# A new written-out order of tasks, and six tiles for output in place of four, in a fused sparse attention and maxout kernel

## The chip, the cores and the metric

The kernel runs on one core of a Trainium2 chip. The core has TensorE (PE: matmuls; PEld is its loading of weights), VectorE (DVE), ScalarE (ACT), GpSimd (POOL) and SyncE (SP), which here only issues DMA transfers. Each engine works through its own instructions strictly in order and waits where data are not ready. The metric is the device time of one execution in microseconds (us); lower is better.

## The reference

Two parts follow each other. The first is attention over 4 batches, 8 heads, 768 positions and a head size of 64. Each query sees the keys closer than 16 positions and, besides, one summary for each block of 32 positions: the largest value of the block's keys, element by element, and the mean of its values.

```python
k_sum = k.reshape(B, H, nb, block, D).max(axis=3)
v_sum = v.reshape(B, H, nb, block, D).mean(axis=3)
scores_l = scale * np.matmul(q, k.transpose(0, 1, 3, 2))
mask_l = np.abs(pos[:, None] - pos[None, :]) < window
scores_s = scale * np.einsum('bhsd,bhnd->bhsn', q, k_sum)
scores_s = scores_s + np.log(block)
scores_l_m = np.where(mask_l, scores_l, -1000000000.0)
scores_all = np.concatenate([scores_l_m, scores_s], axis=-1)
...
return np.matmul(a, v_all).astype(np.float32)      # a: softmax of scores_all
```

Its result, 3072 tokens of 512 numbers, is the input x of a maxout layer with 1024 hidden units:

```python
h1 = x @ w1
h2 = x @ w2
g = np.maximum(h1, h2)
return (g @ w_out).astype(np.float32)
```

All inputs and the output are float32 in HBM; the kernel multiplies in bfloat16.

## The kernel before, in words

**Maxout.** The kernel uses max(h1, h2) = h1 + max(h2 − h1, 0). So it keeps wd = w2 − w1, computes x·wd (*hidden*), takes max(·, 0) on the way out of PSUM (*relu*), and multiplies by w_out. The share of h1 goes through a product w1·w_out, made once (*w1o*, from w1 turned, *w1t*). A batch has three groups of 256 tokens. For each group there are four *hidden* tasks of 8 matmuls (L660), four *relu* tasks, and for each half of 128 tokens an *output*: three steps of 4 matmuls that add into one PSUM bank (L674 with w1o, then L681 twice with w_out), a *copy out* from PSUM to a tile `o` in SBUF (L410 through the helper `copy`), and a *store* from there to HBM (L692). The tiles `o` form a ring, L202; it has four tiles. A copy into a tile must wait until the store that last read it has landed.

**Attention.** For each batch and pair of heads, k and q are loaded in float32 into a landing tile (`land`, a ring of eight; L305), *cast* to bfloat16 (`kqb`), *turned* on TensorE (L434), and *placed* from PSUM into `kx` and `qx` (L410); for k the block maxima (*max*, L454), their copies (*sums*, L461) and a *wrap* (L458) follow on DVE. *Scores* (L501) go to PSUM, *exp* (L515, ACT) to a tile `pb`, and in batches 1 to 3 a *mask* (L509, DVE) clears what is out of the window; in batch 0 TensorE adds the mask itself. v is loaded in two halves (L327), cast to `vb`, and *spread* into `vx` in five pieces (L410, on DVE, POOL, ACT or as a DMA issued by SP); the block means come from matmuls (*means*, L346 and L349) and are copied (*spread means*). *Values* (L543) multiply `pb` by `vx`; *inv* (L549) and *x* (L552) normalise on DVE; x is turned (*turn x*, L575) and copied to `xt` (L410), the input of *hidden*. Weights are loaded by L599 (w1, w2) and L629 (w_out), cast (`w1b`, `wo`), subtracted (`wd`, L607), turned (L618) and copied (`w1t`).

**Names.** A task is named by what it does, then batch, head pair or group: load k12 is the load of k for batch 1, head pair 2; v21 is the second half of v of batch 2; hidden 103 is batch 1, group 0, fourth of four; values 1 30 31 is batch 1 for the units (head pair 3, group 0) and (3, 1); output 021 is batch 0, group 2, second half.

**Order.** There are 679 tasks. Their order is written out as one string, `ORDER` (L20). Each word of it gives the engine by a letter (P = TensorE, A, D, G = POOL, S = SP), the task's number, and after a colon the places that its new buffers take in their rings: `A510:2` runs task 510, the copy of output 021, on ACT into output tile 2. `Plan.run` (L128) walks the string and issues each task on its engine. The string thus sets at once the order on all five engines, which engine does the work where there is a choice, and the PSUM banks and tiles. The planner that searched for it is not part of the kernel; the durations in the calls of `op` are left from it and are not read when the kernel is built. PSUM has eight banks (`banks`); tasks of attention take two, hidden and output tasks one.

All DMAs are issued by SP, on one queue, in the string's order. On it stand the loads, the stores and those spreads that are done as DMAs. In the order before, two pieces and the means of v1, two pieces of v2 and two of v3 are spread by DMA; the others are copies on DVE or POOL.

Of the kernel before, what the change touches and what calls it, by code (L numbers as in the profile page):

```python
# [12 lines left out]
F32 = mybir.dt.float32  # L13
# [7 lines left out]
    "G4:0 D6:0 D0 D2 S36:0,0 S12:1,0 S38:2,0 G5:0 S40:3,0 S13:0 S41:0 S37:0 D77:0 A68:1 D1 G23:0,0,0 "  # L21
    "G32:0,0 S39:0 P79:0,0 G7 G8 D81:0,0 P70:2,0 A92:2 S14:4 G9 A72:2,0 D82:0 P94:4,0 G101:3 S16:5 "
    "A96:1,0 D3 G10 D83 P103:6,0 S42:6 A69:0 D97:1 G102:1 P71:0 S43:7 A76:0 D84 P104:0 D98 D73:0 G78:2 "
    "A109:1 D105:3,0 G93:3 P80:0 A85:2 D75 P95:0 D74 D106:0 A100:3 P86:2 S62:1 P90:6 D99 A87:0 D107 D108 "
    "P88:0 P110:4 A91:1 D15:0,0 D18 P24:2 A89:2 D20 S52:3 P114:6 D21 A22 D19 A25 P112:0 A111:3 D17:0 "
    "S65:0 D26 A28 P33:3 D27 P116:4 D29 A34 A115:4 D30 P126:2 D31 S53:2 D35 A113:5 G45:0 D117:0 P121:6 "
    "D118:0,0 A49:1 D122:1 G48:0 P119:0 D127:2 D123:1,0 P46:4 S146:4,0 A120:0 D128:0 P124:6 A47:1,0 P50:0 "
    "D125 P131:2 D44:0 A64:0 P460:6 S147:0 D51:0 G63:0 P458:7 A461:0 D132:0 P446:4 D55:1 A59:0 D133:0 "
    "P449:5 S150:5,0 D459 P60:0 P56:2 P455:6 D61:0 A57:0 D66:0 P136:0 P452:7 D67:0 S153:6,0 D137:1 P456 "
    "D138:0 S152:0 P134:2 P129:0 D58:0 P447 S151:0 P453 D54:0 A448:0 S154:7 A130:1 P450 D135 G218:0 "  # L30
    "S156:1 A219:1 P464:4 D457:0 G163:1,0,0,0 G245:2 A451:0 D454:0 S148:0,0 P221:0,0 P139:2 P220:0 P476:6 "
    "D11:0 A140:2 D465 S149:0 A222:0,0 P462:5 D477:1 G257:3 A226:0 P480:7 D223:1 G258:1 A246:0 P482:2 "
    "D224 D463 A481 P141:3 D225 P259:0,0 A483 S175:2,0 P260:0 P227:5 D261:2,0 P478:7 A228:0 D142:2 P484:2 "
    "D143:0 A479 G155:0,0 P248:5,0 D262:0 P247:0 P144:3 A253:2 P471:7 D265:1 S170:3,0 A249:1,0 P485 D229 "
    "A145 P472 D263 D251 D250:1 G157:0 P486 P500:0 D487:0 G230:3 S161 P164:1 P489:5 A231:1 S174:0 D160 "
    "S162 A165 P494:6 D159 A501:2 A167 P232:3,0 P233:0 D264 P490 A234:3,0 D166 G187:0,0,0,0 D168 S169 "
    "A238:3 P473 D235:0 S173:4,0 A495 P496:2 S171:0 D236 D252 D237 D474:1 P266:0 A497 P242:3 P491 D158 "
    "S178:6 A243:2 S180:5 P498:6 D492:2 A267:3 S172:0 P239:2 D499 P269:4 P502:7 A240:5 S493 D268 P507:0 "
    "D244 A270:1 D241 P503 D271 P272:1 P284:3 P254:5 D273:0 D285:1 P504 D274:2,0 S176:7,0 A255:4 D286:0,0 "
    "P508 A505:3 D256 P275:1 A295:0 P278:5 G179:0,0 P287:3 D276:2 P466:7 D279:0 A307:2 D277:0 D288:1 P509 "  # L40
    "S177:0 D280:0 G294:3 D289:0 P281:1 G321:1 P467 S475 D282:2 D283:0 S201:1,0 G181:0 P296:5,0 A510:2 "
    "P290:3 P297:0 A298:0,0 P292:1 D291:3 S197:0,0 P468 A302:0 G306:3 D293 P188:0 S200:0 G322:0 P309:3,0 "
    "P323:5,0 S511 P308:0 A469:1 P516:1 D310:3,0 A325:2,0 S506 P514:2 G334:2 D191 A517:1 D311:1 P518:7 "
    "G333:1 A314:3 S194:6,0 D515 G186 P512:1 A519 S184 D185 P335:3,0 P324:0 A513 P336:0 D326:0 P536:2 "
    "S195:0 A329:1 D341:2 S199:3,0 P520:7 A189 A337:1,0 D313 P530:1 S183 D192 A537:2 D312 D339 D327 "
    "P532:5 D328 A531 D338:1 S198:0 A190 P330:3 P315:1 D300 P521 D299:0 G370:3 A316:0 P552:6 D340 D301 "
    "A331:3 D317 P522 D182 A553:0 P525:0 A523:2 D332 P303:1 A533 P345:3 D193 S204:5 P548:6 A304:5 S488 "
    "S196:0 P534:7 A549 S524 D305 P543:5 A535 P318:1 P342:6 P544 A319:2 P526 A343:1 D320 S202:4 P545 "
    "A346:4 S470 D344 P527 A546:3 P357:1 P351:6 A528:0 P354:3 P550:5 D352:0 A371:1 D355:1 S529 D353:1,0 "
    "P538:0 D358:2 G382:0 A551 D359:2,0 A383:2 P554:6 G205:0,0 D356:0 P561:7 A555 D347 P372:1,0 P385:3,0 "  # L50
    "P373:0 A374:2,0 P384:0 G409:3 P562 D378:1 A386:0,0 G397:2 P360:5 D390:0 P348:1 A410:1 P563 G203:0 "
    "D349:0 D361:2 D350:0 P556:3 D564:2 G211:1,0,0,0 S208 G209 P363:1 P557 D362:0 S206 S547 D364:1 P539 "
    "D365:0 P411:4,0 D387:1 P366:6 G207 P412:0 P368:1 A367:0 P558 D369 P540 A398:0 D559:1 P584:6 A413:3,0 "
    "S560 G210 S565 P568:7 A417:3 D585:1 P588:1 D376 D541:0 P602:2 D375:0 S542 P566:3 D569:0 A603:2 D377 "
    "P586:6 D567 P590:4 D389 A587 D414:0 P212:5 P379:2 D214 P400:6,0 D589 P399:0 A380:3 P604:0 D401:1,0 "
    "P570:1 A405:2 D381 P572:2 A213 D388 A605 D402:1 P574:3 A571 D573 A591 P592:6 D216 A215 D403 D404 "
    "P575 D415 D416 D217 P421:0 P394:4 P579:7 A422:0 P576 A395:2 P580 D577:3 P391:0 D396 S578 P406:4 "
    "P418:2 P593 A407:1 P581 A419:5 D408 P594 A582:1 D420 P597:4 A392:4 D423 P606:5 A595:2 D393 P598 A607 "
    "P433:2 P439:0 P424:6 D434:0 P599 D435:0,0 D440:2 P608:5 D425:1 A600:0 D426:1,0 P610:2 D441:0 A609 "
    "P436:3 P427:6 P430:0 P615:5 D428:0 D437:1 D429:0 P611 D438:0 D431:2 P616 D432:0 P444:6 P442:3 A445:3 "  # L60
    "P617 D443 P612 P674:0 D613:3 P644:1 S614 P628:3 A645:0 S601 P660:4 A618:3 P622:6 S619 S583 P669:7 "
    "D623:1 P624:2 P620:1 A625 P664:5 D621 P638:6 P640:2 D639 P626:1 D661:2 D641 P658:6 D627 P633:4 A659 "
    "P642:2 P634 D643 P662:1 P651:6 D663 P646:2 P656:1 P652 A657 P635 P665 A636:0 P653 P629 D654:3 P666 "
    "S655 S637 P647 A667:1 P630 S668 S596 P648 D631:3 P675 S632 A649:0 P670 P676 S650 P671 A677:1 D672:2 "
    "S678 S673 "
# [81 lines left out]
def kernel(  # L147
# [14 lines left out]
    nc = tc.nc  # L162
# [5 lines left out]
    d_model, d_ff = H * D, 1024  # L168
# [5 lines left out]
    op = plan.op  # L174
# [4 lines left out]
    def tiles(name, n, shape, dt):  # L179
        return [const.tile(shape, dt, name=f"{name}{i}") for i in range(n)]  # L180
# [21 lines left out]
    osr = Ring(tiles("o", 4, [128, d_model], F32))  # L202
# [117 lines left out]
    def load_v(b, prio, gap, on):  # L320
# [3 lines left out]
        for n in range(2):  # L324
            f = Buf(land)
            view = lambda f=f: f.ap[:, 0:1536].rearrange("p (h m d) -> p h m d", h=4, d=D)
            op("SP", 3.6, lambda view=view, n=n: nc.sync.dma_start(  # L327
# [266 lines left out]
    def load_w12(half, prio, prio_t):  # L594
        fs = []
        for w in (moe_w1, moe_w2):
            f = Buf(land)
            fs.append(f)
            op("SP", 2.75, lambda f=f, w=w: nc.sync.dma_start(  # L599
                out=wide(f), in_=w.rearrange("(c p) n -> p c n", p=128)[:, :, 512 * half:512 * half + 512]),  # L600
               write=[f], prio=prio, label=f"load w{half}")
        for n in (2 * half, 2 * half + 1):
            split_w12(n, fs, prio + 10 * (n % 2), prio_t)
# [23 lines left out]
    def load_wo(half, prio):  # L627
        f = Buf(land)
        op("SP", 2.75, lambda: nc.sync.dma_start(  # L629
# [152 lines left out]
```

## Time and profile before

| | |
|---|---|
| time, median of 5 runs | 173.75 us (172.97 to 174.65) |
| time of the profiled execution | 172.97 us |
| its span, first to last instruction of the program | 171.2 us |
| mean granted TensorE clock | 0.978 |
| instructions | 5197 |
| read from HBM, written to HBM | 25.17 MB, 6.29 MB |
| chain that ended last | PE 75%, DMA 12%, DVE 5%, SP's queue 4%, ACT 1% of the span |
| load of v, issue to landing (median of 8) | 11.2 us |
| loads of k and of q (median of 16 each) | 7.1 us |

A busy share is the share of the span in which the engine had an instruction. The windows view gives the same for stretches of the span. A wait is named by what released it. Times in the text are from the start of the span. "From start to start" is the time between the starts of two tasks that follow each other on TensorE; since matmuls overlap, this, and not the length of one, is what a task costs there.

### The profile page before, as it was taken

How to read it: one execution, taken by the hardware profiler on the slowest of the kernel's cores; microseconds unless marked ns; L12 is line 12 of the kernel's file. 1: busy time of each engine (PE TensorE's matmuls, PEld its weight loads, DVE VectorE, ACT ScalarE, POOL GpSimd, SP SyncE). 2: the span in 40 equal slices, each digit the busy share in tenths (PEclk: the TensorE clock that was granted, in tenths of full speed). 3: DMA queues.
4: the chain of work that ended last, by engine and by line, in shares of the span. 5: the costliest groups of instructions: out<-in, count | busy, mean ns of one | idle time of the engine just before them, and what ended most of it. 6: DMA issues, size and time to landing. Idle time of an engine off the chain costs nothing.

```text
span 171.2 us, 5197 instructions
## 1 busy us (share of the span) xinstructions
PE 151.4 (88%) x2256; PEld 98.3 (57%) x2256; DVE 114.4 (67%) x204; ACT 92.1 (54%) x126; POOL 43.8 (26%) x63
## 2 busy tenths in 40 slices
PE   0348539999999999979999999999999999999992
PEld 0236427647846556557665654788555657886451
DVE  1657899688799897749996549488965661353110
ACT  2578796418763987059797860816666232110220
POOL 7661037106264001871100559600000000000000
PEclk9999975999999999999999999999999999999999
DMA  5999999999999499999999924540010003300065
GB/s 158 343 331 219 304 372 397 386 375 331 221 265 299 89 286 223 248 382 384 262 199 272 270 79 98 151 146 6 0 65 0 0 4 123 126 0 0 0 245 184
DMA packets 42070, 33.57 MB, mean 196 GB/s; under 512 B 25888, under 2 KB 36032, under 8 KB 42048
## 3 DMA queue, kind: packets, MB, share of 16 engines
q1 hardware_dynamic: 42048, 33.25, 68.8%
q8 instruction: 17, 0.28, 0.7%
q14 instruction: 5, 0.04, 0.1%
HBM read 25.17 MB, written 6.29 MB: 184 GB/s over the span
## 4 chain that ended last, share of the span: by engine, by line
PE 75%; DMA 12%; DVE 5%; SPq 4%; ACT 1%; issue 1%; ACTq 0%
PE banks L660 24%; PE banks L681 23%; PE banks L674 12%; DMA land<-in_v_dram 8%; PE banks L644 4%; DMA out_dram<-o 4%; PE banks L543 4%; PE banks L501 3%; SPq L305 3%; DVE vx L410 3%; PE banks L434 2%; PE banks L575 2%; DVE xs L552 1%; ACT kx L410 1%; PE banks L618 1%
## 5 line engine op out<-in xcount | busy, mean ns | idle before, releaser
L660 PE MATMUL banks<-xt,wd 128*128 128x256 bf16 x384 | 47.4, 276 | 0.2 <-ACT g L406 0.2
L681 PE MATMUL banks<-wo,g 128*128 128x512 bf16 (+1 forms) x200 | 45.5, 371 | 0.0
L660 PEld LDWEIGHTS <-wd 128*128 128x128 bf16 x384 | 37.3, 99 | 8.9 <-issue 0.3
L515 ACT ACTIVATE pb<-banks,bias 128x1024 bf16<-128x1024 f32 x24 | 25.6, 1111 | 7.5 <-PE banks L501 7.2
L681 PEld LDWEIGHTS <-g 128*128 128x128 bf16 x200 | 18.4, 98 | 18.6
L406 ACT ACTIVATE g<-banks 128x512 bf16<-128x512 f32 x29 | 17.0, 601 | 20.9 <-PE banks L660 20.8
L410 POOL CAST kqb<-land 128x768 bf16<-128x768 f32 x19 | 16.5, 880 | 33.8 <-DMA land<-in_k_dram 28.0
L674 PE MATMUL banks<-w1o,xt 128*128 128x512 bf16 (+1 forms) x100 | 24.4, 371 | 0.0
L408 DVE TENSOR_SCALAR g<-banks 128x512 bf16<-128x512 f32 x19 | 12.8, 688 | 11.4 <-PE banks L660 11.3
L434 PE MATMUL banks<-identity,kqb 64*128 64x64 bf16 x384 | 10.6, 202 | 10.6 <-DVE kx L236 5.0
L410 ACT COPY o<-banks 128x512 f32<-128x512 f32 (+1 forms) x14 | 8.0, 570 | 16.8 <-PE banks L681 9.1
L454 DVE TENSOR_REDUCE ks<-kx 128x24 bf16<-128x768 bf16 x16 | 15.1, 947 | 2.1 <-ACT kx L410 2.0
L552 DVE TENSOR_TENSOR xs<-banks,inv 128x512 bf16<-128x512 f32 x24 | 15.8, 680 | 0.3
L434 PEld LDWEIGHTS <-kqb 64*128 64x128 bf16 x384 | 7.8, 101 | 14.3 <-DVE kx L236 5.0
L410 DVE COPY o<-banks 128x512 f32<-128x512 f32 (+1 forms) x11 | 7.3, 664 | 11.4 <-PE banks L681 11.2
L509 DVE TENSOR_TENSOR pb<-pb,mask 128x1024 bf16<-128x1024 bf16 x18 | 12.0, 687 | 3.3 <-ACT pb L515 3.2
L410 ACT CAST kqb<-land 128x768 bf16<-128x768 f32 x12 | 9.9, 836 | 8.0 <-DMA land<-in_k_dram 4.1
L674 PEld LDWEIGHTS <-xt 128*128 128x128 bf16 x100 | 9.3, 98 | 7.7
L410 POOL CAST vb<-land 128x1536 bf16<-128x1536 f32 x6 | 8.9, 1477 | 18.4 <-PE banks L543 13.1
L543 PE MATMUL banks<-vx,pb 128*64 128x65 bf16 x384 | 9.7, 200 | 3.0 <-DVE vx L410 1.4
L543 PEld LDWEIGHTS <-pb 128*64 128x64 bf16 x384 | 7.9, 114 | 7.7 <-issue 7.6
L410 ACT COPY xt<-banks 128x512 bf16<-128x512 bf16 (+1 forms) x6 | 5.2, 874 | 10.9 <-PE banks L575 10.9
(66 smaller groups left out, 155.8 us busy)
## 6 DMA issues: line engine op xcount, KB each, us to landing
land<-in_k_dram SPq DMA_DIRECT2D x16, 384.0 KB, 7.1
land<-in_q_dram SPq DMA_DIRECT2D x16, 384.0 KB, 7.1
land<-in_v_dram SPq DMA_DIRECT2D x8, 768.0 KB, 11.2
out_dram<-o SPq DMA_DIRECT2D x19, 256.0 KB, 3.3
land<-in_moe_w_dram SPq DMA_DIRECT2D x4, 1024.0 KB, 10.9
land<-in_moe_w_out_dram SPq DMA_DIRECT2D x2, 1024.0 KB, 12.6
out_dram<-o SPq DMA_DIRECT2D x4, 224.0 KB, 3.1
vx<-vb SPq DMA_DIRECT2D x2, 396.0 KB, 7.2
```

Of the source, the lines that this page charges most:

```text
L406: nc.scalar.activation(out=o, in_=i, func=ACT.Relu)
L408: nc.vector.tensor_scalar_max(out=o, in0=i, scalar1=0.0)
L410: {"DVE": nc.vector.tensor_copy, "ACT": nc.scalar.copy, "POOL": nc.gpsimd.tensor_copy, "SP": nc.sync.dma_start}[e](out=o, in_=i)
L434: nc.tensor.transpose(out=bank(ps, 2048, BF16)[:, at:at + 64], in_=src.ap[r, j].rearrange("p h d -> p (h d)"), identity=identity[r, r])
L454: op("DVE", 0.95, lambda: nc.vector.tensor_reduce(out=ks.ap[:].rearrange("p (t s) -> p t s", s=2), in_=kt()[:, :, 0:64].rearrange("p t (s ...
L509: nc.vector.tensor_tensor(out=o, in0=o, in1=m, op=ALU.mult)
L515: op("ACT", 1.13, lambda: nc.scalar.activation(out=pb.ap[:].rearrange("p a n -> p (a n)"), in_=bank(ps, 1024), func=ACT.Exp, bias=bias[:], ...
L543: nc.tensor.matmul(out=av()[64 * par:64 * par + 64, c, 2 * u + a, :], lhsT=pb.ap[:, a, at:at + 64], rhs=vx[b].ap[:, 4 * grp + 2 * u + par, ...
L552: op("DVE", 0.69, lambda: nc.vector.tensor_tensor(out=x.ap[:, grp] if g1 == grp else x.ap[:, grp:g1 + 1, hp % 2], in0=av()[:, :, :, 0:D], ...
L660: nc.tensor.matmul(out=bank(ps)[:, 256 * s:256 * s + 256], lhsT=wd[n].ap[:, c, 128 * s:128 * s + 128], rhs=x_rows(b, grp)[:, c, :], start= ...
L674: nc.tensor.matmul(out=bank(ps, hi - lo), lhsT=x_rows(b, grp)[:, c, sl], rhs=w1o[c].ap[:, lo:hi], start=(c == 0), stop=False)
L681: nc.tensor.matmul(out=bank(ps, hi - lo), lhsT=g.ap[:, f, sl], rhs=wo[f // 2].ap[:, f % 2, lo:hi], start=False, stop=(f == FC - 1))
```

## The change

The string `ORDER` is replaced by another for the same 679 tasks; the ring of output tiles grows from four to six. Three durations given to `op` change too (the second load of v of batch 0, the loads of w1 and w2, the load of w_out); they are not read when the kernel is built and alter no instruction.

What moves, besides the order on each engine:
- SP: k and q of batch 0 are loaded in the order k03, k01, k00, q02, q00, q01, k02, q03 (before: k01, k00, k02, k03, q00, q03, q01, q02); v0 and the weights follow in the same order as before. In batch 1, q11, q12 and k11 come ahead of v11 and v10, and q20, q21, k20, q22 and k21 ahead of the spreads of v1. Stores: 011 is issued after k31, 020 and 000 after q33, 001 and 010 only after the loads of v3.
- Spreads by DMA: v14, v13 and means of batch 1 as before; of batch 2 v24, v23, v20, v22 and the means (before v22 and v21); of batch 3 v31, v32, v30 and the means (before v32 and v30). Spread v21 goes from SP to POOL, v24 from POOL to SP.
- Counted over the tasks, SP issues 87 DMAs in place of 82; instructions go from 202 to 196 on DVE, from 125 to 127 on ACT and from 57 to 56 on POOL, and stay 2256 matmuls on TensorE.
- Copies from one engine to another, among them: spread v041 and wo 2 from DVE to ACT, w1b 2 from DVE to POOL, w1b 3 from ACT to DVE, the copy of output 021 from ACT to DVE.

```diff
 ORDER = (
-    "G4:0 D6:0 D0 D2 S36:0,0 S12:1,0 S38:2,0 G5:0 S40:3,0 S13:0 S41:0 S37:0 D77:0 A68:1 D1 G23:0,0,0 "
...
-    "S177:0 D280:0 G294:3 D289:0 P281:1 G321:1 P467 S475 D282:2 D283:0 S201:1,0 G181:0 P296:5,0 A510:2 "
...
+    "G5:0 D6:0 D1 D2 D0 S40:0,0 S36:1,0 S12:2,0 S39:3,0 G23:0,0,0 G4:0 S13:0 S37:0 A101:0 S38:0 G7 "
...
+    "S199:0,0 P296:6,0 P297:0 D510:4 P290:4 S176:0 A298:0,0 P292:0 G322:3 D291:3 P468 A302:0 S186 G321:2 "
...
-    osr = Ring(tiles("o", 4, [128, d_model], F32))
+    osr = Ring(tiles("o", 6, [128, d_model], F32))
...
-            op("SP", 3.6, lambda view=view, n=n: nc.sync.dma_start(
+            op("SP", 3.6 + 0.65 * n * (b == 0), lambda view=view, n=n: nc.sync.dma_start(
...
-            op("SP", 2.75, lambda f=f, w=w: nc.sync.dma_start(
+            op("SP", 2.85, lambda f=f, w=w: nc.sync.dma_start(
...
-        op("SP", 2.75, lambda: nc.sync.dma_start(
+        op("SP", 2.85, lambda: nc.sync.dma_start(
```

## The prediction

> **What bounds the kernel now.** I read the page first, then the windows by stage, the waits, and the timeline around each wait.
>
> ```profile
> span 171.2 us, 5197 instructions
> ...
> PE 151.4 (88%) x2256; PEld 98.3 (57%) x2256; DVE 114.4 (67%) x204; ACT 92.1 (54%) x126; POOL 43.8 (26%) x63
> ...
> PE   0348539999999999979999999999999999999992
> ...
> DMA  5999999999999499999999924540010003300065
> ```
>
> TensorE is nearly full from slice 7 to slice 39, with one dent at slice 18. DMA is full until about 100 us and then nearly idle. The windows put numbers on that (the columns are span of the stretch, then busy us and instructions per engine, granted clock, DMA share, GB/s):
>
> ```profile
> 0.00:28.80 28.80, 13.95 (x341) 10.38 (x341) 19.61 (x42) 19.80 (x23) 12.97 (x34) 0.91 1.01 300
> 28.80:67.70 38.90, 38.90 (x581) 24.07 (x579) 32.69 (x57) 24.74 (x35) 10.59 (x10) 0.98 1.02 280
> 67.70:78.70 11.00, 9.71 (x207) 6.38 (x201) 7.58 (x14) 4.47 (x8) 8.22 (x9) 1.00 1.04 320
> 78.70:100.70 22.00, 21.97 (x352) 14.57 (x351) 17.17 (x29) 17.51 (x26) 3.29 (x4) 1.00 1.06 255
> 100.70:102.70 2.00, 1.59 (x38) 0.79 (x32) 1.07 (x2) 1.90 (x3) 2.00 (x3) 1.00 0.00 0
> 102.70:168.00 65.30, 65.28 (x772) 42.15 (x771) 35.84 (x63) 23.66 (x34) 6.75 (x5) 1.00 0.22 68
> 168.00:171.20 3.20, 0.00 (x0) 0.00 (x0) 0.42 (x1) 0.00 (x0) 0.00 (x0) 0.92 0.40 138
> ```
>
> So there are four parts: a ramp to 28.8 us in which TensorE waits for data, a dense stage to 168.0, within it idle time of 1.3 us in the third row and 0.4 us in the fifth, and a tail of 3.2 us. What the idle time is:
>
> ```profile
> ACT o L410 <- DMA out_dram<-o: 7.5, 3, 4.8
> ...
> PE banks L434 <- ACT qx L410: 0.6, 1, 0.6
> PE banks L346 <- ACT o L410: 0.5, 1, 0.5
> ```
> ```profile
> 73.20 0.59 ACT L410 COPY o<-banks 128x512 f32<-128x512 f32 x1 [4.83 <-DMA out_dram<-o]
> ...
> 73.84 0.52 PE L346 MATMUL banks<-vb,amean 128*32 128x128 bf16 x24 [0.55 <-ACT o L410]
> ...
> 75.24 0.53 PE L434 MATMUL banks<-identity,kqb 64*128 64x64 bf16 x24 [0.60 <-ACT qx L410]
> ```
>
> ScalarE stands 4.83 us for an output tile whose store has not landed; the bank that it would free, and the placements queued behind it, then hold TensorE. Measured from start to start against the usual step of the same pair of tasks, TensorE loses 0.62 us (72.25 to 73.84; an output step followed by small matmuls takes 0.96), 0.77 (74.29 to 75.24 against 0.18), 0.07, 0.33 (77.53 to 78.73 against 0.87) and, by another wait, 0.58 (101.79 to 102.64 against 0.28): 2.4 us after the ramp.
>
> **The change part by part.** *Six output tiles and the stores.* Copy of output 021 moves from ACT tile 2 to DVE tile 4, one of the new tiles, which nothing has used: no store is waited for. The next copies take tile 5 (000, also new) and tile 2 (100), whose store is now issued two loads behind v21, ahead of nine key and query loads. This is what ends the first three losses; the fourth (placement of q31 behind a full DVE) goes with the new order: placements of k31 and q31 stand at 99.8 to 101.7 by my count, the value step that takes their bank at 102.8. Gain 2.4 at most.
>
> *TensorE's own work.* It is the same 232 tasks. In steps from start to start a hidden task is 0.87, an output step 0.86, a turn of k or q 0.18, scores 0.24, values 0.28; a run of small tasks between large ones costs 0.10 at its entry and 0.09 at its exit. From the 34th task on there are 27 such runs before and 28 after: +0.2.
>
> *The ramp.* Eight loads of k and q of 384 KB still precede v, and the six weight loads keep their order and find their landing tiles free, so v01 still lands at 19.95 and the weights at 22.6, 26.1, 28.9, 31.6, 34.2 and 36.9. Behind v01 DVE has:
>
> ```profile
> 19.98 0.96 DVE L410 CAST vb<-land 128x1536 bf16<-128x1536 f32 x1 [0.45 <-DMA land<-in_v_dram]
> 20.97 0.98 DVE L410 COPY vx<-vx 32x2904 bf16<-32x2904 bf16 x1
> 21.97 2.60 DVE L410 COPY vx<-vb 64x1584 bf16<-64x1584 bf16 x4
> 24.60 0.97 DVE L410 COPY vx<-vx 32x2904 bf16<-32x2904 bf16 x1
> ```
>
> One small copy of 0.21 goes to ACT: the chain ends at 25.4 instead of 25.6. Then come two inv (0.22, 0.20) and x for units 00 10 and 01 11 before x 20 30, which ends at 28.0, not 27.4; turn 0.4, then w1t 1 (0.68) stands ahead of xt 001 (0.41): 29.1 against 28.31. The first hidden task starts at 29.1, not 28.8; wd 0 (1.41) ends at 30.5, so the second starts about 30.8 and ends at 31.65, as before (31.64). Then w1b 2 is on POOL: 31.6 + 1.38 = 33.0 against 32.5 when TensorE wants it, a wait of 0.4; against that values 0 02 12 (0.37) now lies ahead of the dense stage, in idle time. After 34 tasks both orders have done the same set: at 37.05 before, 37.15 by this sum: +0.1. Bounds: +1.0 if the three late steps (0.3, 0.8 and 0.4) add instead of hiding behind each other; −1.1 by the clock:
>
> ```profile
> 21.40:25.60 4.20, 1.63 (x37) 1.11 (x36) 4.07 (x6) 4.15 (x5) 1.38 (x1) 0.80 1.00 371
> 25.60:27.00 1.40, 1.00 (x31) 0.86 (x32) 1.36 (x5) 0.34 (x1) 0.79 (x1) 0.50 1.07 411
> ...
> 28.80:30.00 1.20, 1.20 (x10) 0.88 (x7) 1.20 (x2) 1.05 (x1) 1.02 (x1) 0.50 1.05 386
> ```
>
> The first two hidden tasks run half in a clock of 0.50 and take 2.84 us where two later take 1.75. The new order leaves much the same holes there (to 22.9, 23.5 to 24.0, 24.5 to 25.5), so I take no change. [...]
>
> *New waits.* DVE has 196 tasks' instructions in place of 202. Five spreads of v2 and four of v3 are on SP's queue where two and two were, so DVE drops 1.52, 0.97 and 3.17 us for batch 2, and 3.17 for batch 3; POOL takes v21 (2.8). Rows to price them: key loads land every 1.05 us, the two v loads of a batch take 3.0 to 3.8 each, spreads in a full queue 0.4 (165 KB) to 1.9 (396 KB), a lone means spread 4.5 from issue to landing. With TensorE run without a stop from 37.2, due times come from the steps above; what each waits for, and when I find it ready:
> - values 1 30 31 (due 64.3): spread means 1. Two more loads (q21, q20) stand ahead; v10 lands 51.9, the last k21 about 60, the spread 62.5. Margin 1.8.
> - means 20 (due 73.7): v21 lands at 69.8, cast to 71.3. Margin 2.4.
> - turn q22 (due 74.5): place q20, ACT, 73.65. Margin 0.85.
> - scores 2 10 11 and 2 20 21 (due 82.6, 82.8): wrap k21 stands on DVE behind max k22, which waits for place k22 on ACT: 82.0; place q23 82.25. Margin 0.55.
> - hidden 111 (due 84.9): exp 2 10 11, 84.2. Margin 0.7.
> - values 2 20 21 (due 95.0): spread means 2, on SP and behind a means copy that DVE reaches only at 87.6: lands 92.1. Margin 2.9. Behind it on SP stand both v3 loads and stores 001 and 010; copy 121 (102.4) needs the first, which lands about 99.7.
> - hidden 211 (due 107.8): xt 201, 1.43 on ACT, 107.2. Margin 0.6.
> - output 311 (due 139.6): xt 301, 139.0. Margin 0.6.
>
> None comes late, so their price by the sum is zero; but four margins are under 0.9 us, and an instruction behind another in a queue slips easily by 0.2 to 0.6, as the losses of 0.07 to 0.77 before show. I allow 0.4 (bounds 0 and, if most of the gain comes back, 2.4).
>
> *Tail.* Both last half copies are on ACT (0.37) where one was on DVE (0.42); the last two stores follow in the same way: 0.
>
> Sum: +0.1 + 0.2 − 2.4 + 0.4 = −1.7 us. The profiled execution took 172.97 (span 171.2 and 1.8 around it), the fastest of the five; their median is 173.75, 0.8 above. 172.97 − 1.7 = 171.3, and as a median 172.1.
>
> **The rivals.** Differences under 0.5% (0.87 us) can't be told from no change here.
> - *The waits come back elsewhere.* For it: ACT and DVE are back to back between 72 and 85 us in the new order, four margins of 0.55 to 0.85 lie there or just after, and the losses of before have that size. Against it: DVE is lighter by 5.7 us for batch 2. If ACT enters that stretch 1.5 us late, turn q22 loses 0.65, the scores 0.95 and hidden 111 0.8: 2.4 in all, the gain is gone: 173.7 (173.0 to 174.4).
> - *Slower: spread means 2 lands late.* Place: SP's queue at 87.6, behind eleven transfers that follow k23. For it: the slowest spread of before (issue 79.89, landing 89.13, with loads ahead) took 9.2 us; here that is 96.8, a stall of 1.8. From a landing at 97.9 on it decides: a stall of 2.9 in place of the allowance of 0.4 makes 174.6, and all that follows on TensorE stands in order behind it. Against it: by the rows the queue is empty by 87.4. With a landing at 99 the time is 172.1 + 4.0 − 0.4 = 175.7.
> - *The clock stays full in the ramp*, −1.1: 171.0.
> - *The tiles do nothing*, as the order alone would avoid the wait: the same time as the forecast, so it takes no chance from it.
>
> **How the numbers follow.** Forecast (171.3 to 172.9): 0.45. Full clock as well (170.4 to 171.3): 0.13. Waits come back: 0.22, of which 0.02 lies below 172.88 and 0.02 above 174.62. Slower, this and other lateness in the ramp: 0.20 (174.6 to 177). Faster: 0.45 + 0.13 + 0.02 = 0.60; same 0.18; slower 0.22. Leaving out 0.1 at each end gives 170.7 to 175.4.
>
> **What would show it.** Right: no wait of ACT's output copies on stores before 100 us; TensorE's window from 67.7 to 78.7 full; first hidden task near 29, the 34th task's end near 37.1; TensorE's last matmul near 166.3. Wrong: TensorE waiting for means 1 near 64, for place q20 near 74, for wrap k21 or place q23 near 83, for means 2 near 95; or a first hidden task later than 30.

## The result and the profile after

The new order takes 173.35 us (median of 43 executions, 172.14 to 175.28), the kernel before 173.36 us (median of 76, 172.04 to 175.07). The ratio is 0.9993 with a 95% interval of 0.9979 to 1.0008: no change. The forecast of 172.1 us was wrong by 1.2 us. The profiled execution took 173.24 us, its span 171.5.

The page of the new order:

```profile
span 171.5 us, 5208 instructions
...
PE 151.1 (88%) x2256; PEld 98.1 (57%) x2256; DVE 105.3 (61%) x198; ACT 91.5 (53%) x128; POOL 41.7 (24%) x62
...
PE   0155957899999999996999999999999999999992
...
DMA  5999899999999699999974995854000600030175
```

The dent of TensorE at slice 18 is still there, in another shape. The windows over the same stretches as before (span, then busy us and instructions of PE, PEld, DVE, ACT, POOL, granted clock, DMA share, GB/s):

```profile
0.00:28.80 28.80, 13.69 (x328) 9.74 (x330) 18.93 (x40) 19.99 (x24) 11.48 (x33) 0.99 0.98 290
28.80:67.70 38.90, 38.32 (x579) 24.05 (x580) 31.45 (x53) 26.34 (x39) 11.57 (x13) 0.96 1.04 288
67.70:78.70 11.00, 10.08 (x229) 6.49 (x222) 8.03 (x14) 4.89 (x8) 7.61 (x6) 1.00 1.12 333
78.70:100.70 22.00, 21.35 (x297) 14.23 (x296) 15.10 (x33) 12.22 (x17) 3.63 (x6) 1.00 0.97 210
100.70:102.70 2.00, 2.00 (x69) 1.37 (x68) 1.68 (x4) 0.68 (x2) 0.84 (x2) 1.00 1.13 336
102.70:168.00 65.30, 65.30 (x774) 42.08 (x773) 30.15 (x56) 26.63 (x41) 6.54 (x5) 1.00 0.30 90
```

The fifth row is now full (1.59 of 2.00 before). The third gained only 0.4 us, and the fourth lost 0.6. The waits and the timeline of TensorE tell why:

```profile
ACT o L410 <- PE banks L681: 20.2, 9, 7.7
...
PE banks L660 <- issue: 1.6, 1, 1.6
...
PE banks L618 <- POOL w1b L410: 0.6, 1, 0.6
```

```profile
76.75 1.04 PE L660 MATMUL banks<-xt,wd 128*128 128x256 bf16 x8
79.35 1.36 PE L660 MATMUL banks<-xt,wd 128*128 128x256 bf16 x11 [1.57 <-issue]
```

ScalarE's output copies wait for TensorE alone; the 7.5 us in which they waited for stores are gone. In their place TensorE itself stands still in the middle of hidden 113, between two matmuls of one task whose data and bank it already has. The profile finds nothing that it waits for ("issue"). And the dense stage begins later. The chain that ended last, in order of time:

```profile
19.38 12.96 DMA land<-in_moe_w_dram
32.49 1.48 POOL w1b L410
34.66 6.15 PE banks L644 x28
...
77.78 1.57 issue
```

To compare executions I split the time at the start of TensorE's 35th task (up to there both orders have done the same amount of work) and at its last matmul. A start is here that of a task's first weight load, which for a large task behind another large one lies 0.2 us ahead of its first matmul; by first matmuls the 35th task starts at 37.05 and 38.05 us. Losses inside the dense stage are counted from start to start against the usual step, here those over 0.15 us.

| | 35th task starts | from there to the last matmul's end | losses over 0.15 us | last weight lands |
|---|---|---|---|---|
| before | 37.04 | 130.94 | 0.62, 0.78, 0.22, 0.60 | 36.94 |
| new order | 37.84 | 130.53 | 1.73 (hidden 113) | 37.74 |

So the five losses of the prediction (its 0.07 is under the limit here) did go, and one new loss of 1.73 us and a ramp longer by 0.8 us (1.0 by first matmuls) ate the gain.

### The profile page after: what moved, and what is told of

It is laid out like the page before. It is cut to its first block, busy times and chain, and to the rows that moved or that the text cites. A ratio compares the mean times of both kernels' runs of the same rounds, so it can differ in the third digit from the quotient of the medians.

```text
span 171.5 us, 5208 instructions
## 1 busy us (share of the span) xinstructions
PE 151.1 (88%) x2256; PEld 98.1 (57%) x2256; DVE 105.3 (61%) x198; ACT 91.5 (53%) x128; POOL 41.7 (24%) x62
## 4 chain that ended last, share of the span: by engine, by line
PE 77%; SPq 10%; DMA 8%; issue 1%; POOL 1%; ACT 0%; POOLq 0%; ACTq 0%
PE banks L681 25%; PE banks L660 24%; PE banks L674 12%; DMA land<-in_moe_w_dram 8%; SPq L327 5%; PE banks L644 4%; PE banks L543 3%; PE banks L501 3%; PE banks L434 3%; SPq L599 3%; SPq L305 3%; PE banks L575 2%; POOL w1b L410 1%; PE banks L346 1%; PE banks L618 0%
## 5 line engine op out<-in xcount | busy, mean ns | idle before, releaser
L681 PE MATMUL banks<-wo,g 128*128 128x512 bf16 (+1 forms) x200 | 46.4, 371 | 0.0
L406 ACT ACTIVATE g<-banks 128x512 bf16<-128x512 f32 x30 | 17.6, 601 | 17.3 <-PE banks L660 17.3
L408 DVE TENSOR_SCALAR g<-banks 128x512 bf16<-128x512 f32 x18 | 12.1, 689 | 18.8 <-PE banks L660 18.0
L410 POOL CAST kqb<-land 128x768 bf16<-128x768 f32 x17 | 14.0, 834 | 30.3 <-DMA land<-in_q_dram 14.2
L410 ACT COPY o<-banks 128x512 f32<-128x512 f32 (+1 forms) x18 | 10.0, 565 | 20.4 <-PE banks L681 20.2
L434 PE MATMUL banks<-identity,kqb 64*128 64x64 bf16 x384 | 10.1, 202 | 10.2 <-ACT kqb L410 5.9
L410 ACT COPY kx<-banks 128x768 bf16<-128x768 bf16 x12 | 9.7, 805 | 13.1 <-PE banks L434 13.1
L543 PE MATMUL banks<-vx,pb 128*64 128x65 bf16 x384 | 9.0, 200 | 2.9 <-ACT pb L515 1.8
L501 PEld LDWEIGHTS <-kx 64*128 64x128 bf16 x416 | 8.4, 102 | 4.4 <-issue 4.2
```

The lines of the kernel that those rows point to most:

```text
L406: nc.scalar.activation(out=o, in_=i, func=ACT.Relu)
L408: nc.vector.tensor_scalar_max(out=o, in0=i, scalar1=0.0)
L410: {"DVE": nc.vector.tensor_copy, "ACT": nc.scalar.copy, "POOL": nc.gpsimd.tensor_copy, "SP": nc.sync.dma_start}[e](out=o, in_=i)
L434: nc.tensor.transpose(out=bank(ps, 2048, BF16)[:, at:at + 64], in_=src.ap[r, j].rearrange("p h d -> p (h d)"), identity=identity[r, r])
L501: nc.tensor.matmul(**m)
L543: nc.tensor.matmul(out=av()[64 * par:64 * par + 64, c, 2 * u + a, :], lhsT=pb.ap[:, a, at:at + 64], rhs=vx[b].ap[:, 4 * grp + 2 * u + par, ...
```

## The experiments

**Both kernels again.** Nothing edited. For the new order:

> The changed kernel once more, nothing altered, to see what of its first trace comes back. [...] The place is fixed by the count of instructions, so the pause of about 1.6 us inside hidden 113 at about 77.8 us comes back, within 0.7 us. Theory C (chance): the pause was an accident of one execution; it is not there, and TensorE's last matmul ends near 166.6 us, the time is near 171.6 us. Ramp: if the new order itself is slower there, the first hidden task starts again at 29.5 to 30 us and the 35th task at 37.9 to 38.2 us; if the weights only happened to land late, at about 29.0 and 37.2 us.

For the kernel before:

> The kernel before once more. Its five losses after the ramp (2.4 us in the first trace, ScalarE's wait of 4.8 us for a store among them) come back within 0.7 us. For the ramp two theories. R: the new order makes the ramp slower; then the 35th task starts at 36.9 to 37.4 us as in the first trace (the new order had 37.8, and 38.9 when run again). L: the loads land earlier or later by up to 1 us from execution to execution whatever the order, and the first trace of before was a lucky one; then anything from 37 to 38.9 us, mean near 38.

The new order took 173.62 us. The pause is in the same task, 0.87 us by the timeline, 1.03 from start to start:

```profile
76.74 2.13 PE L660 MATMUL banks<-xt,wd 128*128 128x256 bf16 x18
79.74 0.92 PE L660 MATMUL banks<-xt,wd 128*128 128x256 bf16 x7 [0.87 <-issue]
```

Its 35th task started at 38.95 us, the last weight having landed at 38.82. The kernel before took 172.84 us with losses of 0.78, 0.22 and 0.60 (1.6 in all, 130.52 from the 35th task to the end); ScalarE again stood 4.4 us for one store; the 35th task started at 37.33. The pause is no accident, and the ramp is later in the new order both times.

**Moving the borders between blocks of instructions.** The page of DMA queues has a queue named `instruction`, with 17 packets of 16 KB on it (16384 bytes each), where TensorE has 4512 weight loads and matmuls: 265 to a packet, if all of them are TensorE's, as I took them to be. Theory F (fetch) is that each packet brings a block of TensorE's instructions, and that the pause is a wait for one of them.

```profile
q8 instruction: 17, 0.28, 0.7%
```

In the last 60 us, where the DMA is little used (a share of 0.30 from 102.7 to 168.0 us), the packets of the new order start every 218 to 286 of these instructions, about 250. I took it that a block is asked for 250 instructions ahead of the one behind which TensorE stops, and call that place its border. This is an estimate from these counts: no record shows the asking, and in the same trace other packets start from 1.9 us ahead of the border so counted to 4.3 us behind it. In the new order the block in question would be asked for at about 72.9 us (72.7 by 250 exactly); its packet started at 76.6 and ended at 77.73; TensorE stood still from 77.8 us on and went on at 79.35. To move that border without moving any work or transfer, weight loads that nobody uses are put in front:

```diff
         make_identity(nc, identity[:])
+        for _ in range(80):
+            nc.tensor.ldweights(identity[0:64, 0:64])
...
                                             identity=identity[r, r])
+                for _ in range(32 if b == 0 and n == 0 else 0):
+                    nc.tensor.ldweights(identity[0:64, 0:64])
```

With 64 loads (none in front, 16 in each turn of k):

> 64 weight loads that nobody uses are added to TensorE's program in the first 10 us, where it waits for data; no transfer and no order changes. [...] The block that was used up in 4.9 us (72.9 to 77.8 us) becomes one that is used up in 2.8 us (72.4 to 75.2 us). If the fetch again needs about 6.5 us from the border to the first new matmul, the pause moves ahead of 75.5 us and lasts 3.7 instead of 1.6 us: time about 175.4 us (174.5 to 176). Theory H (something in hidden 113 itself, its data or its bank): the pause stays in hidden 113 with 1.6 us, time 173.3 us.

With 208 (as in the diff):

> 208 weight loads that nobody uses are added to TensorE's program in the first 10 us; no transfer and no order changes. Theory F: the borders lie 208 instructions earlier in the work; the block in question is then used up in 7.2 us (73.3 to 80.5 us), the one before it in 5.4 us (67.6 to 73.0 us). No pause in hidden 113, at most one of 0 to 0.5 us near 73 us; TensorE's last matmul 1.1 to 1.7 us earlier; time 171.7 us (171.5 to 172.3), if the loads themselves do not lengthen the ramp (at most 0.5 us). Theory H: the pause stays in hidden 113 with 1.6 us, time 173.3 us.

Measured: 173.08 us (10 executions, ratio to before 0.9981, 0.9943 to 1.0019) and 172.99 us (10, ratio 0.9966, 0.9925 to 1.0007). Hidden 113 and the three hidden tasks next to it run through in both (32 matmuls in a row); first 64, then 208:

```profile
76.14 3.67 PE L662 MATMUL banks<-xt,wd 128*128 128x256 bf16 x32
```

```profile
76.58 3.67 PE L664 MATMUL banks<-xt,wd 128*128 128x256 bf16 x32
```

Theory H (something in hidden 113 itself) is out: the task, its data and its neighbours are the same, and the pause is gone. The times of the two runs are not clearly lower (both intervals reach 1); that the pause costs time is shown further down. My form of theory F missed too: with 64 loads I expected a pause of 3.7 us near 75.5 and there was none: that packet started about at the border so counted, at 73.22, where the one of the new order started about 3.75 us after it. From the 35th task to the last matmul these runs took 129.07 and 128.77 us in place of 130.53; their ramps were long, 38.48 and 38.92 us (the second because the added loads themselves delayed the first turns by 1 us).

**Less traffic.** The loads of k and q of batch 3 bring 16 of 128 partitions:

```diff
-                out=view(), in_=src[b, 2 * hp:2 * hp + 2].rearrange("h (p j) d -> p h (j d)", j=J)),
+                out=view()[0:16 if b == 3 else 128],
+                in_=src[b, 2 * hp:2 * hp + 2].rearrange("h (p j) d -> p h (j d)", j=J)[0:16 if b == 3 else 128]),
```

> The new order, but the loads of k and q of batch 3 bring only 16 of 128 partitions (left out: the rest of k and q of batch 3, so its results are not the reference's). Eight loads of 384 KB between 68 and 90 us become 48 KB; TensorE's instructions and every order stay. Theory F in the form that the fetch of a block stands in the DMA queues behind data: the block asked for at about 73 us starts less than 1.5 us later instead of 3.1 to 3.75 us, and there is no pause in hidden 113. If the delay has nothing to do with the other transfers: it starts 3 to 4 us later and the pause of 0.9 to 1.7 us stays.

One execution: 171.40 us. In the window the DMA moves 212 and 137 GB/s at a share of 0.80 and 0.70 (in the new order 391 and 289 GB/s at 1.06 and 1.10), and TensorE does not pause:

```profile
72.00:76.00 4.00, 3.84 (x153) 3.02 (x154) 2.51 (x3) 2.25 (x4) 3.93 (x4) 1.00 0.80 212
76.00:80.00 4.00, 3.95 (x34) 3.20 (x33) 2.86 (x4) 3.94 (x9) 3.94 (x4) 1.00 0.70 137
```

The packet for the block at the same border started about 2.0 us after it, by the same estimate, and ended at 75.90. I had expected less than 1.5; in the six traces with the border at this place and full loads it was some 3.1 to 3.75. Less traffic brought the block earlier, and with it the pause went. That the fetch stands in line behind data is what this fits; the waiting itself is not recorded.

**The ramp.** Every engine gets the order of before up to TensorE's 34th task (the first 146 words of the string are those of before), the rest stays the new order, with six tiles; 14 buffers of the rest take another place in their ring, since the tiles are free in another sequence.

```diff
 ORDER = (
-    "G5:0 D6:0 D1 D2 D0 S40:0,0 S36:1,0 S12:2,0 S39:3,0 G23:0,0,0 G4:0 S13:0 S37:0 A101:0 S38:0 G7 "
...
+    "G4:0 D6:0 D0 D2 S36:0,0 S12:1,0 S38:2,0 G5:0 S40:3,0 S13:0 S41:0 S37:0 D77:0 A68:1 D1 G23:0,0,0 "
...
```

> Every engine's order up to the 34th task of TensorE from the kernel before, the rest from the new order, with six tiles. Theory R (the new ramp costs 0.8 us or more): the 35th task starts at 36.9 to 37.4 us and the time falls by 0.8 to 1.1 to about 172.4 us against 173.35 of the new order; the pause of 1.0 to 1.7 us in hidden 113 stays, since the borders of the blocks lie at the same instructions. Theory L (the loads scatter, order or not): the 35th task at 37 to 38.9 us, time 173.3 us like the new order.

Measured 172.37 us (12 executions; ratio 0.9967, 0.9936 to 0.9998). The 35th task starts at 37.31, the pause is there (1.22 us). The forecast of theory R holds. Once more, for its trace, and then timed on another chip:

> The ramp of before and the rest of the new order without unused weight loads, once more for its trace (the first: 172.37 us, pause of 1.2 us in hidden 113, 35th task at 37.3 us). Theory F: the pause in hidden 113 comes back with 0.7 to 1.7 us; the first matmul after it starts 1.4 to 1.7 us after the packet of the fetch ends.

> The ramp of before and the rest of the new order with six tiles, without added loads, timed again beside the other: first 172.37 us against 173.44 of before (ratio 0.9967, interval 0.9936 to 0.9998). If that was no accident, 172.2 to 172.6 us and a ratio of 0.994 to 0.997, with a pause of 0.7 to 1.7 us in hidden 113; if it was, 173.3 us.

172.26 us in the one execution, and 172.66 us (12; ratio 0.9958, 0.9933 to 0.9983), just above the range that I gave. Pauses 1.16 and 1.15 us, 35th task at 36.95 and 37.79 us. With the ramp of before the new order is 0.8 to 1.1 us (0.3 to 0.4%) faster than the kernel before, and so than the new order as it was, which equals that.

What makes the new ramp long? Two trials took one part of it each, the order of the first eight loads, put into the kernel before, and POOL's hide_t before hide, put into the new order:

> The kernel before, with only its first eight loads in the new order (k03, k01, k00, q02, q00, q01, k02, q03). In the four traces with the new order so far the DMA moves only 170 to 250 GB/s between 4.5 and 6.5 us, where before moves 320 to 400, and the last weight tile lands at 37.4 to 38.8 us in place of 36.7 to 37.5. Theory A (the order of the first loads makes the dip): it appears here, about 200 GB/s between 4.5 and 6.5 us, the third load lands at 7.5 to 8.5 us, the last weight at about 38 us. Theory B (what POOL, ScalarE and VectorE do at that time makes it): no dip, the last weight near 37.0 us.

> The new order with one exchange: POOL fills hide_t before hide, as the kernel before does. Theory A: the dip of the DMA to about 200 GB/s between 4.5 and 6.5 us stays. Theory B, in the form that POOL's work makes the dip: it goes, 320 GB/s or more, and the last weight lands near 37.1 us. The pause in hidden 113 stays in any case (0.9 to 1.7 us).

The first had a dip of the DMA (260, 170 and 240 GB/s between 5 and 6.5 us), its eighth load landed at 12.96 us as in the new order (12.8 to 14.1; with the loads of before 11.7 to 12.6), but its last weight landed at 37.11, early. (Its 177.78 us say nothing on the question: the other engines were left in the order for other loads, and TensorE waited.) In the second the dip stayed, and the last weight landed at 38.87; the pause was 1.16 us. So, by one trace each, POOL's order is not the cause, and the order of the loads alone does not suffice. Over all traces the last weight lands at 37.0 us on average in the twelve with the ramp of before (36.4 to 37.5) and at 38.2 in the six with the new one (37.4 to 38.9). The chip does not make this difference: on one and the same chip it landed at 37.4 to 38.8 in three traces of the new ramp and at 37.0 to 37.2 in four of that of before. Which of the other changes in the new ramp makes the loads late, I could not settle.

**Six tiles alone.** The order of before, each of its 25 output copies taking the next of six tiles, as far as that tile is free:

```diff
-    osr = Ring(tiles("o", 4, [128, d_model], F32))
+    osr = Ring(tiles("o", 6, [128, d_model], F32))
...
-    "S177:0 D280:0 G294:3 D289:0 P281:1 G321:1 P467 S475 D282:2 D283:0 S201:1,0 G181:0 P296:5,0 A510:2 "
...
+    "S177:0 D280:0 G294:3 D289:0 P281:1 G321:1 P467 S475 D282:2 D283:0 S201:1,0 G181:0 P296:5,0 A510:4 "
...
```

> The order of before, word for word, with six output tiles taken in turn. If the store wait is the cause of the losses at 73 to 79 us, ScalarE no longer waits 4.8 us and 1.4 to 1.8 us of the 2.4 go (the loss at 102 stays): time 171.6 to 172.0 us against 173.4. If TensorE now runs into the late block of instructions, as the new order does (asked for at 71.8 us, used up by about 78 us without the stalls, landed at 75.3 us before, so 2.7 us to spare), a pause takes up to 1 us of it: 172.6 us. If the tiles do nothing: 173.4 us.

173.25 us (12 executions; ratio 1.0004, 0.9965 to 1.0043): none of the three. The losses at 73 to 75 us did go, but a late store holds a later copy and TensorE behind it, which costs 0.75 us, and the pause for instructions appears with 0.38 us:

```profile
97.07 0.58 ACT L410 COPY o<-banks 128x512 f32<-128x512 f32 x1 [1.98 <-DMA out_dram<-o]
```

```profile
97.71 1.02 PE L674 MATMUL banks<-w1o,xt 128*128 128x512 bf16 x3 [0.59 <-ACT o L410]
```

The loss at 102 us stayed (0.56), and this execution's 35th task started at 37.94. More tiles without moved stores hand the wait on.

**The ramp of before with moved borders.** First with 64 loads, placed as above:

> As the kernel with the ramp of before and the rest of the new order, and besides 64 unused weight loads for TensorE in the first 10 us, which took the pause in hidden 113 away. All five losses of before, the pause and, by theory R, the slower ramp are gone: last matmul near 165.8 us, time 171.3 us (171.0 to 171.8). By theory L the ramp gives nothing: 172.2 us. If the pause was no loss on the path: no better than without the loads.

173.31 us (12; ratio 0.9997, 0.9961 to 1.0033): missed. Hidden 113 is free of it, but now the pause stands at 75.3 us, before the last matmul of turn q22, where I had worked out the border for 64 loads, and it passes 0.77 us on; another 0.61 is lost behind it to a late cast of k23:

```profile
74.57 0.70 PE L434 MATMUL banks<-identity,kqb 64*128 64x64 bf16 x35
75.84 0.36 PE L434 MATMUL banks<-identity,kqb 64*128 64x64 bf16 x13 [0.57 <-issue]
...
82.28 0.35 PE L434 MATMUL banks<-identity,kqb 64*128 64x64 bf16 x12 [0.42 <-POOL kqb L410]
```

(These are 48 matmuls, the turns of k21, q21, q22 and k22.) In the run with the long ramp TensorE came to this place 0.8 us later and the block was there in time.

This run settles what the pause goes by. Count TensorE's weight loads and matmuls, the unused ones too: in all eight traces with a pause it stops behind the same instruction, the 2239th. Without added loads this lies inside hidden 113 in the new order (six traces) and ahead of the last matmul of hidden 100 in the order of before with six tiles; with 64 it lies in turn q22. Three tasks with other data and banks, and one count.

Then with 208 loads, spread over what I took for TensorE's idle time before 27 us (56 in front, 12 to 18 after each turn of k, 5 after three turns of q, 30 after the matmuls of the second half's means, 51 after values 0 20 30):

> The ramp of before, the rest of the new order with six tiles, and 208 unused weight loads for TensorE, put where it waits for data before 27 us. By theory F the borders of the blocks then lie where the run with 208 showed no pause at all: no loss over 0.3 us after the 35th task, which starts at 37.0 to 37.7 us; the last matmul 128.8 us after that, near 166.1 us; time 171.5 us (171.2 to 172.0). If the weight loads take time on the path: the 35th task at 38 us or later and 172.3 us. If the place of the borders is no cause: a pause as in the run with the ramp of before, 172.4 us.

The profiled execution is what was worked out: 171.22 us, no loss, the last matmul at 166.42. The median of 12 was 173.26 (ratio 0.9992, 0.9958 to 1.0026). Three more traces of the same kernel were to show the difference:

> The kernel with the ramp of before and 208 unused weight loads again, for its trace alone. Its profiled execution took 171.22 us, with no loss after the ramp, but its median was 173.26 us. Theory S (the loads land earlier or later by an us from execution to execution, and the fetches of instructions with them): an execution near 173.3 us shows the last weight at 38 us or later, or a pause on a fetch of 0.5 us or more, together 1.5 to 2 us. If neither is there in an execution of 173 us, the cause is another.

> The same again, for a second trace: by theory S time less 171.2 us equals the lateness of the 35th task over 37.5 us plus the pauses, within 0.3 us.

> The same again, for a third trace: by theory S time less 171.2 us equals the lateness of the 35th task over 37.5 us plus the pauses, within 0.3 us.

They took 174.01, 173.59 and 172.54 us. None has a loss over 0.18 us after the ramp, and in none are the last weights late (36.97 to 37.20 us), but the 35th task starts at 40.19, 39.94 and 38.88. So the sum of theory S holds within 0.2 us, but not its reason. The added loads are part of the reason (the good execution, then the first of the three):

```profile
24.46 0.69 DVE L560 TENSOR_TENSOR xs<-banks,inv 128x512 bf16<-128x512 f32 x1
24.58 1.98 PEld L179 LDWEIGHTS <-identity 64*64 64x64 bf16 x51
26.57 0.23 PEld L583 LDWEIGHTS <-xs 64*128 64x128 bf16 x8
```

```profile
25.85 0.69 DVE L560 TENSOR_TENSOR xs<-banks,inv 128x512 bf16<-128x512 f32 x1
26.15 2.79 PEld L179 LDWEIGHTS <-identity 64*64 64x64 bf16 x51
28.96 0.24 PEld L583 LDWEIGHTS <-xs 64*128 64x128 bf16 x8
```

The values before the 51 loads end at 24.6 or at 26.1 us, depending on when v landed and was spread, and the x that TensorE is to turn next is ready at 25.15 or 26.54. Both times the loads stand ahead of this turn (L583), on the path: without them TensorE waits 0.37 us at this place (ramp of before), and they take 1.98 us at a granted clock of 0.74, or 2.79 at 0.50 (not the 5.7 that the expectation below names). In the good execution the early v hid this. A second part is the clock: it is back at 1.00 at 32.4 us in the good execution and at 35.3, 34.7 and 32.6 in the other three. The third of these starts the turn at 28.98 like the first, and its 35th task 1.3 us earlier.

**The version that beats both.** As before, but with 144 loads, all before 13.5 us (56 in front, 14 to 18 after the turns of k, 8 after three turns of q):

> The ramp of before, the rest of the new order, and 144 unused weight loads, all before 13.5 us, where the clock is full and TensorE waits for loads (none between 20 and 29 us, where 51 of them took up to 5.7 us at half clock). The borders then stand at about 70.0 and 74.7 us; the block between them lasts 4.5 us. By theory F with a fetch that starts 1.7 us after it is asked for, as at 70 us in the runs with 208, the first matmul of the next block can start at 74.3 us: no pause, or one up to 0.5 us, and none in hidden 113. 35th task at 37.0 to 37.6 us, last matmul 166.0 to 166.7 us, median 171.4 to 172.0 us. If the fetch comes as late as in the new order (3.1 to 3.75 us): a pause of 1.4 to 2 us near 74.5 us, 172.9 us.

171.69 us (6 executions, 170.85 to 172.06; ratio to before 0.9907, 0.9875 to 0.9938), faster than the kernel before by 0.6 to 1.3%, where the same kernel without the added loads took 172.66 (12) beside it on the same chip. So the pause lay on the path. The 35th task started at 37.92 and the last matmul ended at 166.99, both 0.3 us behind what I had expected; the largest loss after the ramp was 0.17 us. DMA is as full as ever in the window, and TensorE does not pause:

```profile
72.00:76.00 4.00, 3.84 (x152) 2.77 (x152) 2.66 (x4) 1.97 (x3) 3.94 (x4) 1.00 1.06 397
76.00:80.00 4.00, 3.95 (x35) 3.27 (x34) 2.58 (x3) 3.94 (x9) 2.33 (x3) 1.00 1.10 304
```

All traces but that with the order of the loads, the longest dense stage first:

| run | 35th task starts | from there to the last matmul's end | pause on instructions, start to start | profiled execution |
|---|---|---|---|---|
| before | 37.04 | 130.94 | | 172.97 |
| new order | 37.84 | 130.53 | 1.73 | 173.24 |
| before again | 37.33 | 130.52 | | 172.84 |
| ramp of before, second trace | 36.95 | 130.52 (0.42 of it behind a copy of w1o) | 1.16 | 172.26 |
| six tiles alone | 37.94 | 130.38 | 0.38 (by the timeline) | 173.42 |
| ramp of before | 37.31 | 130.28 | 1.22 | 172.37 |
| ramp of before, 64 loads | 37.64 | 130.24 | 0.77 | 172.71 |
| ramp of before, third trace | 37.79 | 130.21 | 1.15 | 172.78 |
| new order, hide_t first | 38.96 | 129.94 | 1.16 | 173.77 |
| new order again | 38.95 | 129.81 | 1.03 | 173.62 |
| new order, 64 loads | 38.48 | 129.07 | none | 172.40 |
| ramp of before, 144 loads | 37.92 | 129.07 | none | 171.79 |
| ramp of before, 208 loads, four traces | 37.53 to 40.19 | 128.85 to 129.02 | none | 171.22 to 174.01 |
| new order, small loads of batch 3 | 37.78 | 128.78 | none | 171.40 |
| new order, 208 loads | 38.92 | 128.77 | none | 172.55 |

Without a pause the new order's dense stage takes 128.8 to 129.1 us, whatever took the pause away; with one 129.8 to 130.5, where that of before takes 130.5 to 130.9. All six traces with the border where the new order has it and full loads have the pause in hidden 113; none of the eight with a moved border has it there.

## Why the prediction was wrong, by its steps

**Six tiles and the stores, −2.4: right.** No output copy waits for a store in the whole trace; all five losses are gone. The new order needed its moved stores for this: with the tiles alone the wait came back later.

**TensorE's own work, +0.2: right.** From the 35th task to the last matmul I had 129.2 us (37.1 to 166.3), with the allowance in it; the traces without a pause have 128.8 to 129.1. Before, without its losses, it is 128.65 (130.94 less 2.22 and 0.07); the first trace of the new order without its pause 128.80.

**The ramp, +0.1: mis-sized; the late steps add.** The sum let three late steps hide behind each other and kept +1.0 as a bound in case they add. They add. DVE went as worked out (x 20 30 ended at 28.07 against 28.0 forecast; xt 001 at 29.32 against 29.1). But from 28.12 us on TensorE had no gap, and values 0 02 12, which I had put in idle time, stood ahead of the first hidden task, which started at 29.74 in place of 29.1 (before: 28.80). Then came w1b 2, which I had expected at 33.0. The load that it casts landed at 32.35 in place of 31.56, and POOL took 1.47 us:

```profile
32.49 1.47 POOL L410 CAST w1b<-land 128x1024 bf16<-128x1024 f32 x1 [1.15 <-DMA land<-in_moe_w_dram]
34.02 0.64 PE L618 MATMUL banks<-identity,w1b 64*128 64x64 bf16 x32 [0.58 <-POOL w1b L410]
```

In the five traces of the new ramp whose first turns were not delayed by added loads, TensorE's turn of w1b 2 starts 0.05 to 0.06 us after this cast and the 35th task 3.82 to 3.83 after that, 5.5 us after the landing; TensorE stood idle for the cast in three of them (0.46 to 1.06 us), in the other two it came just then. (That the last weight lands 0.05 to 0.13 us ahead of the 35th task in these five is no wait: it goes into wd, which this task does not read.) The measured term is +0.8 in the first trace and, against the eight traces with the ramp of before and without the 208 loads, +0.9 on average, near the upper bound. Whether w1b 2 on ACT or DVE, as before, would have sufficed was not tried.

The end of the ramp of before goes with the clock and not with the loads. In one of its traces the first hidden task started at 28.84 and the last weight landed early, at 36.43 us, and yet the 35th task started at 37.79 in place of 37.04. In both traces the granted clock had fallen, and it was back later in this one (before, then the third trace with the ramp of before):

```profile
30.80:32.60 1.80, 1.80 (x14) 1.13 (x13) 1.01 (x2) 1.46 (x2) 0.00 (x0) 1.00 1.08 394
30.80:32.60 1.80, 1.80 (x9) 1.14 (x8) 1.42 (x3) 1.50 (x2) 0.00 (x0) 0.50 1.08 393
```

In the seven traces of this ramp without 144 or 208 loads the 35th task starts at 36.95 to 37.33 where the clock is back by 31.7 us, and at 37.64 to 37.94 where it is back at 32.6 to 32.8. For the new order I took no change of the clock, and −1.1 as the bound if it stayed full. It did neither: it stayed up 4.3 us longer (to 28.2 us, before to 23.9), then fell all the same, for 3.4 us in place of 6.8. The rows of the new order:

```profile
25.60:27.00 1.40, 0.50 (x24) 0.46 (x26) 1.35 (x4) 1.40 (x2) 1.28 (x1) 1.00 1.02 383
27.00:28.80 1.80, 1.37 (x52) 0.99 (x50) 1.63 (x4) 1.64 (x3) 1.07 (x1) 0.84 1.05 387
28.80:30.00 1.20, 1.20 (x34) 1.07 (x35) 1.11 (x2) 1.20 (x3) 0.32 (x1) 0.50 1.05 387
```

**New waits, +0.4: the list was right, and the wait that came was not on it.** None of the eight margins was used up: means 1 landed at 63.5 us for values that started at 64.7, means 2 at 95.1 for 97.4. The allowance stood for slips of data. This is the step that failed: it put the wait for TensorE's own instructions at nothing, a resource that my list of queues did not have, though its queue stands in the profile's DMA part. That wait came, with 1.0 to 1.7 us. By my estimate of the border it is a consequence of the gain. In the kernel before, the block at this border lasted 7.9 us (71.8 to 79.7), 1.3 of them idle time that was to go; in the new order, without them and with the small matmuls closer together, it lasts 4.9 us (72.9 to 77.8), and its packet, which started some 3.1 to 3.75 us after the border in the six traces there, was late.

In each of the eight traces with a pause 0.4 to 1.7 us were lost by it; in the new order the DMA was full there (a share of 1.12 from 67.7 to 78.7 us).

**Tail, 0: right** (3.2 us before, 3.1 after). **The base:** 173.75 was the median of five; over 76 it is 173.36, so 0.4 of my 0.8 between profiled execution and median was chance.

The sum of the profiled execution, 171.3 forecast and 173.24 measured: the ramp 0.7 more, the pause 1.7, the unused allowance −0.4, together 2.0 of the 1.9 to be explained. The rival "waits come back elsewhere" had the right outcome (the gain is gone) and the wrong place; by its own terms it comes to 172.1 − 0.4 + 2.4 = 174.1, not 173.7, and five of the margins, not four, lie under 0.9; the rival "spread means 2 lands late" had the right kind of question and 2.3 us to spare.

## What to carry to other kernels

When a change takes waits away from a full engine, ask how fast it will then use up its instructions as well as its data: count them against the packets of the instruction queue (here one of 16 KB to about 250), estimate from the count where each block begins, and look at what the DMA is doing there; a few unused instructions placed where the engine surely waits can move a border, and gained 0.6% here. A ramp in which a load, a copy and the clock each come close to being last is costed from several executions, since one trace can be 1 us lucky; and before a landing is called the cause, look whether the task that starts behind it reads what landed. Filling "idle" time is safe only where the wait is longer than the filler in every execution.

## What the runs showed of the hardware

The first matmul after a pause on instructions started a nearly constant time after the end of the packet on the instruction queue, at whatever time and place it stood:

| run | packet ends | TensorE goes on | between |
|---|---|---|---|
| new order | 77.73 | 79.35 | 1.62 |
| new order again | 78.26 | 79.74 | 1.48 |
| new order, hide_t first | 78.37 | 79.88 | 1.51 |
| ramp of before (three traces) | 77.02, 76.96, 77.45 | 78.56, 78.45, 78.98 | 1.54, 1.49, 1.53 |
| ramp of before, 64 loads | 74.43 | 75.84 | 1.41 |
| six tiles alone | 77.60 | 79.13 | 1.53 |

So in these eight traces 1.41 to 1.62 us lie between the end of the packet and the first matmul after the pause. In the two runs in which TensorE passed the 2239th instruction without a pause though its packet brought the same block, it did so 1.63 (small loads of batch 3) and 1.54 us (new order, 64 loads) after the packet's end: just in time. In these traces the pause has no releaser ("issue"); it is known by standing inside a task.

Between 22 and 30 us the granted clock falls to 0.50 once in every trace, for 3.4, 6.8 or 10.2 us. In the 10 us ahead of the fall TensorE's longest gap between matmuls was 1.83 us in the kernel before and 1.12 in the first trace of the new order. One and the same ramp, that of before, had the low clock for 6.8 us in six traces and for 10.2 in one. What makes the clock fall, no run here shows.
